# The kernels' transform of an S4D layer: last stage on sixteen 32x32 tiles, and its order on TensorE tied to the output projection's

## The chip, the cores and the metric

The kernel runs on one core of a Trainium2 chip. The metric is device time of one execution in microseconds, as the median of the runs shown. The profile's engine names are used: PE (TensorE's matmuls), PEld (its weight loads), DVE (VectorE), ACT (ScalarE), POOL (GpSimd), SP (SyncE, which here only starts transfers). All tensors in device memory are float32.

## The reference, cut to what matters

The input `x` is 2048 positions x 640 channels. Four layers run one after the other, attention and S4D in turn, with the same weights the second time:

```
x = x + MHA(LN(x))      # 32 heads of 20 channels, softmax, then @ wo (640 x 640)
x = x + S4D(LN(x))
x = x + MHA(LN(x))
x = x + S4D(LN(x))

S4D(u):  K[d, l] = 2 Re sum_n C[d,n] dt[d] exp(A[d,n] dt[d] l)   # 640 channels x 2048 positions, 128 states
         y = irfft(rfft(u, 4096) * rfft(K, 4096))[:2048] + u * D_skip
```

`K` hangs on the weights alone. It is computed once, its transform is computed once, and both S4D layers read that transform.

## The kernel before, in words

**Attention.** For each pair of heads, ScalarE's exponentials (`pt<-S`) stand between the score matmuls (`S`, line 858) and the value matmuls (`pa`, line 892). Results are copied to `oc`, normalised with `db` and stored to device memory in rows (`ot<-oc`, issued by POOL). In the first layer a generator, `kgen`, makes `K` (`kd` in device memory) piece by piece beside attention. The list `rest` holds the pieces of work that prepare the output projection; they run in attention's last stretch.

**Output projection** (`out_proj`). There are 16 rows `s` of 128 positions. A row is loaded as `otl`, split into a high and a low part (`oh`, `ol`), and multiplied with the split weights `woh`, `wol` in 30 matmuls of 128x320: ten of `ol` x `woh` (line 1307), then twenty of `oh` x `woh` and `wol` (line 1312), into two PSUM banks `po`. DVE adds a bank to `x`. Behind it comes the layer norm `ln_u` of a row or a group of rows, which makes `uh` and `ul`, the split input of the convolution.

**Kernels' transform** (`ktransform`, first layer only). This is the Fourier transform of `K`, in five blocks of 128 channels. It is a generator too. `filler` holds it, and `weave(n)` runs `n` of its pieces, up to its next `yield`. In a block:
1. `kl`, 128 channels x 2048 positions, is loaded from `kd`, `D_skip` is added to its first element, and 16 transposes (`pkt<-kl`, line 1244) turn it, split into halves `ktrh` (ACT) and `ktrl` (DVE).
2. First stage: eight groups of twelve f16 matmuls (`pkx`, line 1256), copied to `kx1`.
3. 32 transposes (`pkt<-kx`, line 1264), four at a time, copied with a scale to `kxt`.
4. Last stage: for every four transposes one f32 matmul of 128x512 (`pkf`, line 1272) with the matrix `f`. Two shuffles on DVE spread its 16-row halves over the partitions of `kn[0]` and `kn[1]`, ACT multiplies `kn[1]` by a sign (`sgn`), and for every second one two stores of 512 KB go to `kha` and `khb`.

Its constants `f`, `sgn` and `skip` and the tiles `ktr`, `kx1` lie in the pool `f1`, opened when the generator first runs; `kl`, `kxt` and `kn` have two buffers each in `f2`. A pool that takes memory which another pool has left waits for the last use of that pool.

**Order.** In row 2 of the output projection `weave(1000)` emits the whole transform at once. The scheduler of the framework then places each instruction on its engine by dependency and priority, so that on PE the transform and the projection's rows mix freely. `chain` (with `tie`) is how the program fixes an order by hand: an instruction that is tied stands behind the one tied before it on its engine. In before only `kgen` uses it. An engine runs its instructions strictly in the order in which they were placed.

**Convolution** (`ssm`). It transforms `uh`, `ul` (`psx`, line 1384, copied by ACT to `x1`), multiplies by `ka` and `kb`, which 160 transfers of 256 KB read from `kha` and `khb` in the two layers, and transforms back.

Of the kernel before, what the change touches and what calls it, by code (L numbers as in the profile page):

```python
# [21 lines left out]
P = 128  # L22
# [65 lines left out]
def mha_s4d_kernel(ctx, tc, x_in, wqkv, wo, lar, aim, cr, ci, ldt, dsk,  # L88
                   c_e1, c_eb, c_f2, c_fa, c_sel, c_lv, c_id, c_sg, c_e16, c_f16, c_id16, c_dn, out, parts="asas", general=None):
    nc = tc.nc  # L90
# [26 lines left out]
    wd = dram.tile([P, 3, len(LV), D], F32, name="wd")  # L117
    kha = dram.tile([P, D // 4, P], F32, name="kha")
    khb = dram.tile([P, D // 4, P], F32, name="khb")
    qs = dram.tile([2, D, L], F16, name="qs")  # L120
# [68 lines left out]
    def chain(ins):  # L189
        last[0] = tie(ins, last[0])  # L190

    def kgen():
# [954 lines left out]
    def prefetch(x, rest):  # L1147
# [42 lines left out]
        return x, c, woh, wol, w2  # L1190
    ups = []

# [15 lines left out]
    SWAP = list(range(16, 32)) + list(range(16))  # L1208
    DUP0 = list(range(16)) * 2
    DUP1 = list(range(16, 32)) * 2  # L1210

    def by_channel(x1, i2):
        return x1[:, :, i2].rearrange("p g (s c) -> p s g c", c=4)

    def ktransform(e1):

        c = ExitStack()
        c1 = c.enter_context(tc.tile_pool(name="f1", bufs=1))
        c2 = c.enter_context(tc.tile_pool(name="f2", bufs=2))
        f2 = c1.tile([P, P], F32, name="f2")  # L1220
        sy.dma_start(f2, c_f2)
        sgn = c1.tile([P, 1], F32, name="sgn")
        sy.dma_start(sgn, c_sg)

        skip = c1.tile([P, NCT], F32, name="skip")
        sy.dma_start(skip, dsk)

        def load(b):
            kl = c2.tile([P, L], F32, name="kl")
            sy.dma_start(kl, kd[b * P:b * P + P, :])  # L1230
            return kl
        kls = [load(0)]

        def unit_load(b):
            kl = kls.pop()
            if b + 1 < NCT:
                kls.append(load(b + 1))
            ve.tensor_add(kl[:, 0:1], kl[:, 0:1], skip[:, b:b + 1])
            hi, lo = (c1.tile([P, NI, P], F16, name=f"ktr{n}") for n in "hl")
            klv = kl.rearrange("d (p i) -> d i p", i=NI)  # L1240
            for i4 in range(4):
                pt = pst("T", [P, 4, P], F32, tag="T", name="pkt")
                for i in range(4):
                    te.transpose(pt[:, i, :], klv[:, 4 * i4 + i, :], ident)
# [3 lines left out]
                yield  # L1248
            x1 = c1.tile([P, 32, NI // 2, 16], F32, name="kx1")
            for i2 in range(NI // 2):  # L1250
                ps = pst("X", [P, 2, 2, P], F32, tag="X", name="pkx")
                for i in range(2):
                    s = 2 * i2 + i
                    for r in range(2):
                        for n, (e, m) in enumerate(((0, hi), (0, lo), (1, hi))):
                            te.matmul(ps[:, r, i, :], e1[:, e, s, r, :], m[:, s, :], start=(n == 0), stop=(n == 2))
                (ve.tensor_copy if i2 % 4 == 1 else se.copy)(by_channel(x1, i2), ps.rearrange("p r i (g c) -> p (r i) g c", c=4))
                yield
            prev = None
            for q in range(9):  # L1260
                if q < 8:
                    pt = pst("T", [P, 4, P], F32, tag="T", name="pkt")
                    for g in range(4):
                        te.transpose(pt[:, g, :], x1[:, 4 * q + g].rearrange("p i s -> p (i s)"), ident)
                    xt = c2.tile([P, 512], F32, name="kxt")
                    se.activation(xt, pt.rearrange("p g k -> p (g k)"), AF.Copy, scale=ksc[:, 1:2])
                if prev is not None:
                    g0 = b * 32 + 4 * (q - 1)
                    if q % 2:
                        kn = [c2.tile([P, 2, 512], F32, name=f"kn{s}") for s in range(2)]  # L1270
                    px = pst("F", [P, 512], F32, tag="F", name="pkf")
                    te.matmul(px, f2, prev, start=True, stop=True)  # L1272
# [3 lines left out]
                    if q % 2 == 0:  # L1276
                        for s, dst in enumerate((kha, khb)):
                            sy.dma_start(dst[:, g0 - 4:g0 + 4, :].rearrange("p g k -> p (g k)"),
                                         kn[s].rearrange("p q k -> p (q k)"))
                prev = xt  # L1280
                yield
        for b in range(NCT):
            yield from unit_load(b)
        c.close()

    def out_proj(x, woh, wol, rows, first, ln, load):
# [10 lines left out]
        feed()  # L1297
        due = []
        to_come = {s: 0 for s in range(NI)}
        for s, c0, c1 in rows.left + [e[0] for e in rows.loaded + first]:  # L1300
            to_come[s] += 1
        while first:
            (s, c0, c1), oh, ol = first.pop(0)
            pos = [pst("M", [P, 512], F32, tag="mm", name="po")[:, :320] for _ in range(2)]
            for hf in range(2):
                for ct in range(c0, c1):
                    te.matmul(pos[hf], ol[:, ct, :], woh[:, ct, 320 * hf:320 * hf + 320], start=(ct == c0), stop=False)  # L1307
            feed()
            for hf in range(2):
                for ct in range(c0, c1):  # L1310
                    for m in (woh, wol):
                        te.matmul(pos[hf], oh[:, ct, :], m[:, ct, 320 * hf:320 * hf + 320],  # L1312
                                  start=False, stop=(ct == c1 - 1 and m is wol))
# [17 lines left out]
        while due:  # L1331
            ln(*due.pop(0))


# [14 lines left out]
    def ssm(x, uh, ul, consts, last):  # L1349
# [19 lines left out]
        with ExitStack() as c:  # L1369
# [198 lines left out]
    def seq(x, general):  # L1568

        stats = None  # L1570
        for n in range(0, len(parts), 2):
            with ExitStack() as c:
# [9 lines left out]
                if n == 0 and not general:  # L1582
                    psum(c3, M=2, T=2, F=2)
                else:
# [47 lines left out]
def _constants():  # L1632
# [13 lines left out]
    for s, o, m in ((0, 0, C), (1, 0, S), (0, 1, -S), (1, 1, C)):  # L1646
        fa[:, s, :, :, o] = np.einsum("hli,cd->hlcid", m.reshape(4, 4, 16), e4)
    f2 = f2.reshape(2, NI // 2, 2, 4, P).transpose(1, 0, 2, 3, 4)
    sg = np.zeros((4, 2, 16, 1))
    sg[:, 0], sg[:, 1] = -1.0, 1.0  # L1650
# [5 lines left out]
    cs = dict(c_e1=e1.reshape(P, -1), c_eb=eb.reshape(P, -1), c_f2=f2.reshape(P, P), c_sg=sg.reshape(P, 1),  # L1656
              c_fa=fa.reshape(P, -1), c_sel=sel.reshape(P, -1), c_lv=lv, c_id=np.eye(P))
    cs = {n: np.ascontiguousarray(a.astype(np.float32)) for n, a in cs.items()}
    for n, a in (("c_e16", e1), ("c_f16", f2)):
# [10 lines left out]
_ORDER = ["x_in", "wqkv", "wo", "lar", "aim", "cr", "ci", "ldt", "dsk",  # L1670
          "c_e1", "c_eb", "c_f2", "c_fa", "c_sel", "c_lv", "c_id", "c_sg",
          "c_e16", "c_f16", "c_id16", "c_dn"]
# [30 lines left out]
```

## Time and profile before

| | |
|---|---|
| Median of 3 runs | 2675.46 us (2673.86 to 2678.34) |
| The profiled execution | 2680.85 us |
| Its span, and its mean granted clock | 2679.1 us, 0.996 |
| PE busy | 2530.0 us, 94% of the span |
| ACT busy | 2368.7 us, 88% |
| DVE busy | 1516.0 us, 57% |
| POOL busy | 827.7 us, 31% |
| Stage of the change: first `po` to first `psx` | 1102.90 to 1273.59 us |

How to read it: a busy share is a mean over stages with different limits, and matmuls overlap, so that a busy PE need not be at its peak. The 40 slices of the page are 67 us each; the stage of the change is in slices 17 to 20, counted from 1. In a row of instructions stand start and duration in us, engine, line, operation, output and inputs, and how many follow one another (x8); in brackets the idle time before it and what ended it. In a group stand busy time and mean ns, then idle time before and its releasers.

### The profile page before, as it was taken

Reading aid. Unit: us, or ns where it says so; the run is one execution under the profiler, and the core shown is the slowest. Engines: PE = TensorE matmul, PEld = TensorE weight load, DVE = VectorE, ACT = ScalarE, POOL = GpSimd, SP = SyncE. Lnnn points to the kernel's source line nnn. Section 1 sums busy time; section 2 is a strip of 40 time slices with the busy share of each in tenths; the row PEclk is TensorE's granted clock in tenths of the full one; section 3 lists DMA queues with packets and bytes.
Section 4 is the critical chain, followed back from the end, with each engine's and each line's share of the span. In section 5 each row is a group of like instructions: output and inputs, shape, how many; then the busy total and the mean of one; then the engine's idle time right before and its main releaser. Section 6 shows DMA issues by size and latency. Waiting matters only on the chain.

```text
span 2679.1 us, 116332 instructions
## 1 busy us (share of the span) xinstructions
PE 2530.0 (94%) x51106; PEld 1425.0 (53%) x51106; DVE 1516.0 (57%) x3451; ACT 2368.7 (88%) x2793; POOL 827.7 (31%) x1256
## 2 busy tenths in 40 slices
PE   7899999999999998899998999999999998999898
PEld 3445444444444443678896444454444443444788
DVE  8687777886855994477776333232233221154865
ACT  7889999999999999676655799999999999999564
POOL 1123323333323334301672122222222222222376
PEclk9999999999999999999999999999999999999999
DMA  6513222322221224364542121121121113222465
GB/s 210 181 49 86 67 76 55 87 55 76 52 61 49 54 68 155 110 233 162 189 151 69 40 59 50 50 58 47 45 65 38 54 30 93 69 67 60 145 190 162
DMA packets 186580, 242.18 MB, mean 90 GB/s; under 512 B 43376, under 2 KB 128976, under 8 KB 184400
## 3 DMA queue, kind: packets, MB, share of 16 engines
q1 hardware_dynamic: 150048, 188.35, 21.8%
q0 software_dynamic: 36016, 46.30, 7.0%
q8 instruction: 403, 6.60, 1.0%
q14 instruction: 113, 0.93, 0.1%
HBM read 158.50 MB, written 76.01 MB: 88 GB/s over the span
## 4 chain that ended last, share of the span: by engine, by line
ACT 52%; PE 25%; issue 10%; DVE 6%; DMA 3%; POOL 1%; SPq 0%; ACTq 0%; DVEq 0%; POOLq 0%
ACT pt L78 50%; PE pa L892 4%; PE psv L1419 3%; PE psy L1429 3%; PE S L858 3%; PE psx L1407 2%; PE m L611 1%; PE psx L1384 1%; PE po L1312 1%; DMA kop<-ks 1%; PE pst L1394 1%; PE pkf L1272 1%; DVE ktab L78 1%; PE po L1307 1%; PE pq L764 1%
## 5 line engine op out<-in xcount | busy, mean ns | idle before, releaser
L78 ACT ACTIVATE pt<-S 128x1024 f32<-128x1024 f32 x2048 | 1928.6, 1032 | 41.4 <-PE S L858 29.2
L892 PE MATMUL pa<-pt,V 64*32 64x512 f32 x16384 | 1100.9, 590 | 1.4 <-DVE oc L78 1.2
L858 PE MATMUL S<-qop,kop 61*32 61x512 f16 x16384 | 882.9, 381 | 85.2 <-ACT pt L78 68.4
L858 PEld LDWEIGHTS <-kop 61*32 61x32 f16 x16384 | 366.7, 89 | 741.1 <-issue 622.4
L892 PEld LDWEIGHTS pa<-pt,V 64*32 64x32 f32 x16384 | 315.1, 106 | 74.6 <-issue 9.7
L78 POOL DMA_DIRECT2D dn<-oc x252 | 124.5, 501 | 670.6 <-DVE oc L78 643.8
L78 DVE TENSOR_SCALAR qc<-m 128x512 f32<-128x512 f32 (+1 forms) x68 | 46.8, 689 | 303.6 <-PE m L611 303.6
L78 POOL DMA_DIRECT2D db<-dn x252 | 128.0, 514 | 135.1 <-DMA dn<-dr 132.1
L78 DVE COPY oc<-pa 128x512 f32<-128x512 f32 x64 | 44.1, 690 | 199.6 <-PE pa L892 191.9
L611 PE MATMUL m<-xh,wh 64*32 64x512 f16 x2560 | 147.9, 379 | 5.5 <-DVE qc L78 5.5
L78 POOL DMA_DIRECT2D ot<-oc x256 | 130.4, 516 | 71.6 <-DVE oc L78 42.8
L611 PE MATMUL m<-xh,wl 64*32 64x512 f16 x2560 | 148.1, 377 | 0.0
L611 PE MATMUL m<-xl,wh 64*32 64x512 f16 x2560 | 146.7, 376 | 0.0
L611 PEld LDWEIGHTS <-wh 64*32 64x32 f16 x5120 | 92.9, 93 | 78.4 <-issue 36.4
L78 ACT COPY xt<-pst 128x1024 f16<-128x1024 f16 x80 | 81.6, 1022 | 47.2 <-PE pst L1394 47.0
L1412 POOL TENSOR_TENSOR t<-t,kb 128x512 f32<-128x512 f32 x80 | 102.0, 1276 | 67.6 <-DVE t L78 66.7
L78 POOL DMA_DIRECT2D dn<-dr x63 | 35.3, 560 | 248.8 <-DVE dr L78 236.4
L78 DVE TENSOR_SCALAR V<-m 128x160 f32<-128x160 f32 x64 | 20.7, 324 | 158.5 <-PE m L577 158.5
L78 DVE TENSOR_TENSOR kb<-ktab 128x512 f32<-128x512 f32 x160 | 107.7, 692 | 0.0
L577 PEld LDWEIGHTS <-xh 128*128 128x128 f16 x960 | 79.7, 98 | 47.0 <-issue 31.6
L1413 POOL TENSOR_TENSOR t<-t,t 128x512 f32<-128x512 f32 x78 | 99.3, 1273 | 8.5 <-DVE t L78 2.6
L329 PEld LDWEIGHTS m<-kb,ka 128*32 128x32 f32 x3840 | 61.0, 109 | 72.1 <-issue 55.3
(305 smaller groups left out, 4020.7 us busy)
## 6 DMA issues: line engine op xcount, KB each, us to landing
ka<-kha SPq DMA_DIRECT2D x80, 256.0 KB
kb<-khb SPq DMA_DIRECT2D x80, 256.0 KB
db<-dn POOLq DMA_DIRECT2D x252, 64.0 KB, 2.6
kop<-ks SPq DMA_DIRECT2D x176, 80.0 KB
kpw<-wd POOLq DMA_DIRECT2D x60, 192.0 KB, 4.7
qop<-qs SPq DMA_DIRECT2D x256, 40.0 KB
ot<-oc POOLq DMA_DIRECT2D x256, 40.0 KB, 3.0
kha<-kn SPq DMA_DIRECT2D x20, 512.0 KB
```

What stands on the lines that cost most here:

```text
L78: made = f(out, *a, **k)
L329: chain(te.matmul(ps[32 * j:32 * j + 32, c8, :], a[n][:, ch, :], b[n][:, dd, :], start=(n == 0), stop=(n == 2), tile_position=(0, 32 * j)))
L577: chain(te.matmul(ps[:, :n], a_[:, ct, sl], m[:, ct, :], start=(k == 0), stop=(k == 14)))
L611: chain(te.matmul(ps[r][32 * t:32 * t + 32, :], a_[rows, ct, 32 * u:32 * u + 32], m[rows, ct, 512 * v:512 * v + 512], start=(k == 0), stop ...
L764: te.matmul(pq, a_[:, ct, :], m[:, ct, sl], start=(n == 0), stop=(n == 14))
L858: chain(te.matmul(S[32 * t:32 * t + 32, 512 * r:512 * r + 512], kt_[rows, kc + 32 * t:kc + 32 * t + 32], qt[rows, :], start=True, stop=Tru ...
L892: chain(te.matmul(pa[r][32 * j:32 * j + 32, :], V[rows, kt, VP * h:VP * h + 32], pts[j // 2][rows, 512 * (j % 2):512 * (j % 2) + 512], sta ...
L1407: te.matmul(px, f2[:, f, :], xt[:, k, :], start=(n == 0), stop=(n == 2))
L1412: ge.tensor_mul(t2, t2, kb)
L1413: (ge if g0 else ve).tensor_add(t1, t1, t2)
L1419: te.matmul(pv[:, g].rearrange("p r i c -> p (r i c)"), t1[:, g * P:g * P + P], fa, start=True, stop=True)
L1429: te.matmul(py[:, i, :], eb[:, 4 * i4 + i, r, :], v[:, r, 4 * i4 + i].rearrange("p g c -> p (g c)"), start=(r == 0), stop=(r == 1))
```

## The change

- **Last stage.** The matrix `f` becomes two matrices of 32x32, one for `kha` and one for `khb`, which already hold the doubling and the sign. For each block, each half `t` and each of the two, `ends` runs 16 matmuls of 32x32 tiles (`tile_position`) with 512 columns each into four PSUM banks (tags F0 to F3, one buffer each). DVE copies two banks and ACT two, into two `kn` tiles of 512 KB, each stored by one transfer. The shuffles, the sign multiplication and the load of `sgn` go. There are 20 `ends` in all.
- **Layouts.** `kx1` is laid out so that the transposes read every 32nd element. Channels are taken in the order (c g) instead of (g c): `kl` is loaded in four transfers of 32 partitions. `kha` and `khb` have a new shape, and the convolution's loads `ka`, `kb` read pieces of 512 B where they read pieces of 2 KB.
- **`kl`** has one buffer, `kl0`, in the pool `wo1`. Block 0 is loaded in attention's last stretch (from `rest`), each next one after the second half of the by-time transposes of the block before (`by_time(b, 1)`).
- **Copies.** Half of the `kx` copies go to DVE (a quarter before), and every fourth `kxt` copy too (none before).
- **Order on PE.** All the transform's matmuls and transposes are tied, and so are the projection's while the transform lives. After every seventh `po` matmul one piece of the transform is woven in (`mm`). `weave(1000)` moves from row 2 to behind the last layer norm. There are 480 `po` matmuls, so 68 pieces are woven, and the transform has 70.
- **PSUM.** In this stage 2 + 4 banks (M, F0 to F3) in place of 2 + 2 + 2 (M, T, F), beside the two of X, which the transposes now share with `pkx`.
- **Kernel generator.** One `yield` more for each `reduce_max`, and `bound` is queued behind `load_powers(2)`, with key 3 instead of 1.

```diff
     def kgen():
...
         for n, t in enumerate((ld["cr"], ld["ci"], skip)):
+            yield
             ve.reduce_max(big[:, n:n + 1], t, axis=AX.X, apply_absolute_value=True)
...
-        slow.append((1, bound))
         load_powers(2)
+        slow.append((3, bound))
...
         if rest:
+            kl0[:] = [w1.tile([P, L], F32, name="kl")]
+            rest.append(lambda: load_kl(0))
...
+    def load_kl(b):
+        for ch in range(4):
+            sy.dma_start(kl0[0][32 * ch:32 * ch + 32, :],
+                         kd[b * P:b * P + P, :].rearrange("(g c) l -> c g l", c=4)[ch])
...
-        f2 = c1.tile([P, P], F32, name="f2")
-        sy.dma_start(f2, c_f2)
-        sgn = c1.tile([P, 1], F32, name="sgn")
-        sy.dma_start(sgn, c_sg)
+        f2 = c1.tile([P, 2, 32], F32, name="f2")
+        sy.dma_start(f2, c_f2.rearrange("p (s m) -> p s m", s=2))
         skip = c1.tile([P, NCT], F32, name="skip")
-        sy.dma_start(skip, dsk)
+        sy.dma_start(skip, dsk.rearrange("(g c) n -> c g n", c=4))
...
+        def by_time(b, h):
+            kl = kls[0]
+            if h == 0:
+                ve.tensor_add(kl[:, 0:1], kl[:, 0:1], skip[:, b:b + 1])
+                hl[:] = [c1.tile([P, NI, P], F16, name=f"ktr{n}") for n in "hl"]
...
+            for i4 in (2 * h, 2 * h + 1):
...
+                    transpose(pt[:, i, :], klv[:, 4 * i4 + i, :], ident)
...
+            if h and b + 1 < NCT:
+                load_kl(b + 1)
...
-                (ve.tensor_copy if i2 % 4 == 1 else se.copy)(by_channel(x1, i2), ps.rearrange("p r i (g c) -> p (r i) g c", c=4))
+                (ve.tensor_copy if i2 % 2 else se.copy)(x1[:, :, i2].rearrange("p c s g -> p s c g"),
+                                                        ps.rearrange("p r i (c g) -> p (r i) c g", c=4))
+                if i2 % 2:
+                    yield
...
+            def ends(t, xt, s, dst):
+                px = [pst("F", [P, 512], F32, tag=f"F{ch}", name=f"pkf{ch}") for ch in range(4)]
+                for ch in range(4):
+                    rows = slice(32 * ch, 32 * ch + 32)
+                    for g in range(4):
+                        matmul(px[ch][32 * g:32 * g + 32, :].rearrange("p (q k) -> p q k", k=P), f2[rows, s, :],
+                               xt[rows, :, g, :], start=True, stop=True, tile_position=(32 * ch, 32 * g))
+                for h in range(2):
+                    kn = c2.tile([P, 2, 4, P], F32, name=f"kn{s}")
+                    for ch in range(2):
+                        (se.copy if ch else ve.tensor_copy)(kn[:, ch], px[2 * h + ch].rearrange("p (q k) -> p q k", k=P))
+                    sy.dma_start(dst[2 * b + t][:, 2 * h:2 * h + 2], kn)
+            xts = [c2.tile([P, 4, 4, P], F32, name="kxt") for t in range(2)]
+            steps = [(turned, 0, xts[0], 0), (turned, 0, xts[0], 1), (ends, 0, xts[0], 0, kha),
+                     (turned, 1, xts[1], 0), (ends, 0, xts[0], 1, khb), (turned, 1, xts[1], 1),
+                     (ends, 1, xts[1], 0, kha), (ends, 1, xts[1], 1, khb)]
+            if b + 1 < NCT:
+                steps.insert(7, (by_time, b + 1, 0))
+                steps.append((by_time, b + 1, 1))
...
-                    te.matmul(px, f2, prev, start=True, stop=True)
-                    for s in range(2):
-                        ve.stream_shuffle(kn[s][:, (q - 1) % 2, :], px, [DUP0, DUP1][s])
-                    se.activation(kn[1][:, (q - 1) % 2, :], kn[1][:, (q - 1) % 2, :], AF.Copy, scale=sgn)
...
     def out_proj(x, woh, wol, rows, first, ln, load):
...
+        def mm(*a, **k):
+            if filler[0] is None:
+                te.matmul(*a, **k)
+                return
+            matmul(*a, **k)
+            many[0] += 1
+            if many[0] % 7 == 0:
+                weave(1)
...
-                if s == 2:
-                    weave(1000)
...
         while due:
             ln(*due.pop(0))
-
+        weave(1000)
...
-                sy.dma_start(ka, kha[:, g0:g0 + 4, :].rearrange("p g k -> p (g k)"))
-                sy.dma_start(kb, khb[:, g0:g0 + 4, :].rearrange("p g k -> p (g k)"))
+                for t, src in ((ka, kha), (kb, khb)):
+                    sy.dma_start(t.rearrange("p (g k) -> p g k", k=P),
+                                 src[g0 // 16].rearrange("(g a) c q k -> (a c) g q k", g=4)[:, :, q % 4])
...
-                    psum(c3, M=2, T=2, F=2)
+                    psum(c3, M=2, F=1)
```

More of the change, by code (lines that the diff above doesn't have):

```diff
@@ L190, in chain, with matmul, transpose @@
         last[0] = tie(ins, last[0])
+    def matmul(*a, **k):
+        chain(te.matmul(*a, **k))
+    def transpose(*a, **k):
+        chain(te.transpose(*a, **k))
     def kgen():
@@ new lines, in block, with turned @@
+                            matmul(ps[:, r, i, :], e1[:, e, s, r, :], m[:, s, :], start=(n == 0), stop=(n == 2))
+                (ve.tensor_copy if i2 % 2 else se.copy)(x1[:, :, i2].rearrange("p c s g -> p s c g"),
+                                                        ps.rearrange("p r i (c g) -> p (r i) c g", c=4))
+                if i2 % 2:
+                    yield
+            def turned(t, xt, h):
+                for q in (2 * h, 2 * h + 1):
+                    pt = pst("X", [P, 4, P], F32, tag="X", name="pkt")
+                    for g in range(4):
+                        transpose(pt[:, g, :], x1[:, :, :, :, 16 * t + 4 * q + g].rearrange("p c i s -> p (c i s)"), ident)
+                    if q == 3:
+                        ve.tensor_scalar_mul(xt[:, q], pt, ksc[:, 1:2])
+                    else:
+                        se.activation(xt[:, q], pt, AF.Copy, scale=ksc[:, 1:2])
@@ L1282, in ktransform @@
+        for h in range(2):
+            by_time(0, h)
+            yield
         for b in range(NCT):
-            yield from unit_load(b)
+            yield from block(b)
         c.close()
@@ L1306, in out_proj @@
                 for ct in range(c0, c1):
-                    te.matmul(pos[hf], ol[:, ct, :], woh[:, ct, 320 * hf:320 * hf + 320], start=(ct == c0), stop=False)
+                    mm(pos[hf], ol[:, ct, :], woh[:, ct, 320 * hf:320 * hf + 320], start=(ct == c0), stop=False)
             feed()
@@ L1311, in out_proj @@
                     for m in (woh, wol):
-                        te.matmul(pos[hf], oh[:, ct, :], m[:, ct, 320 * hf:320 * hf + 320],
-                                  start=False, stop=(ct == c1 - 1 and m is wol))
+                        mm(pos[hf], oh[:, ct, :], m[:, ct, 320 * hf:320 * hf + 320],
+                           start=False, stop=(ct == c1 - 1 and m is wol))
                 xs = x[:, s, 320 * hf:320 * hf + 320]
                 ve.tensor_add(xs, xs, pos[hf])
-                if s == 2:
-                    weave(1000)
             to_come[s] -= 1
```

69 lines of the change are left out of this document (22 added, 47 removed).

## The prediction

> **What bounds the kernel now.** I read the page's 40 slices first, then busy time by stage, then the groups of instructions of the stage, then the chain and single instructions at its ends.
>
> ```profile
> ACT  7889999999999999676655799999999999999564
> 1102.90 1.73 PE L1307 MATMUL po<-woh,ol 128*128 128x320 f32 x10
> 1273.44 0.31 PE L1312 MATMUL po<-wol,oh 128*128 128x320 f32 x1
> 1273.59 0.23 PE L1384 MATMUL psx<-uh,e1s 128*128 128x128 f16 x1
> 1103.00:1133.00 30.00, 28.30 (x184) 26.92 (x184) 21.44 (x54) 11.78 (x17) 15.34 (x22) 1.00 0.49 154
> 1133.00:1253.00 120.00, 118.34 (x960) 91.71 (x961) 91.95 (x250) 92.85 (x150) 8.81 (x7) 1.00 0.57 216
> 1253.00:1274.00 21.00, 21.00 (x146) 20.39 (x146) 15.16 (x44) 8.56 (x14) 5.83 (x4) 1.00 0.15 50
> ```
>
> ScalarE sets the pace while it stands at 9 (attention's exponentials); it falls to 5–7 in slices 17 to 22. Into that gap falls the stage of the change: the first output projection with the kernels' transform, from the first `po` at 1102.90 to the first `psx` at 1273.59, 170.7 us. The three window rows (columns: length, then PE, weight loads, DVE, ACT, POOL with counts, granted clock, DMA share, GB/s) show PE full in it: 167.6 of 171 us, clock 1.00. The stage ends when PE has done its work; DVE has 128.6 us, ACT 113.2.
>
> PE's time per instruction comes from starts, since the ends of overlapping ones are modelled:
>
> ```profile
> 1190.37 1.09 PE L1264 MATMUL pkt<-ident,kx 128*128 128x128 f32 x8
> 1191.22 0.39 PE L1312 MATMUL po<-woh,oh 128*128 128x320 f32 x1
> 1148.37 0.86 PE pkf L1272 x2
> 1230.91 1.35 PE pkx L1256 x24
> 1248.20 2.92 PE po L1312 x20
> L1272 PE MATMUL pkf<-kxt,f 128*128 128x512 f32 x80 | 41.3, 608 | 0.0
> ```
>
> Eight transposes take 0.85 us to the next start (0.109 each over the stage), 24 `pkx` 1.35 (0.056), 20 `po` 2.92 (0.147), one last-stage matmul (two records: 80 records are 40 instructions) 0.86. Work: 480 x 0.147 = 70.6, 480 x 0.056 = 26.8, 240 x 0.109 = 26.2, 40 x 0.865 = 34.6, together 158.2. So 12.5 us of the 170.7 are waits.
>
> **The change part by part.**
>
> *Last stage.* 40 matmuls become 20 groups (`ends`) of 16 tiles, which fill four banks each. The nearest rows are attention's, where tiles of 64x32 run together:
>
> ```profile
> 2384.10 0.41 PE L858 MATMUL S<-qop,kop 61*32 61x512 f16 x8
> 2384.31 1.06 PE L892 MATMUL pa<-pt,V 64*32 64x512 f32 x16
> 2385.17 0.41 PE L858 MATMUL S<-qop,kop 61*32 61x512 f16 x8
> 2385.51 0.41 PE L1067 MATMUL m<-wol,oh 128*128 128x320 f32 x1
> 2386.30 0.41 PE L858 MATMUL S<-qop,kop 61*32 61x512 f16 x8
> ```
>
> Eight f32 tiles (16 records) take 0.86, as long as one full matmul. Sixteen take 0.865 if all run together, 1.72 in two lots; I take 0.865, since eight cost no more than one. Going from small tiles to full ones and back costs: from 2385.17 to 2386.30 are 1.13 us for an `S` group (0.21, from 2384.10 to 2384.31) and four projections (4 x 0.147 = 0.59), so 0.33 for the two switches. The Trainium skill, "TensorEngine Tiling (Array Packing)", Key Properties, says that a change of tiling mode drains TensorE; the 0.33 us agree, and it speaks against the change. An `ends` thus costs 1.20, twenty 23.9 against 34.6.
>
> *DVE and ACT.*
>
> ```profile
> L78 DVE STREAM_SHUFFLE kn<-pkf 128x512 f32<-128x512 f32 x80 | 54.2, 737 | 0.0
> L78 ACT ACTIVATE kn<-kn,sgn 128x512 f32<-128x512 f32 x40 | 28.3, 721 | 1.5 <-DVE kn L78 0.9 <-DVE va L78 0.2
> L78 ACT ACTIVATE kxt<-pkt,ksc 128x512 f32<-128x512 f32 x40 | 26.6, 677 | 8.8 <-PE pkt L1264 8.8
> L78 ACT COPY kx<-pkx 128x512 f32<-128x512 f32 x30 | 17.4, 584 | 6.4 <-PE pkx L1256 6.3
> L78 DVE COPY kx<-pkx 128x512 f32<-128x512 f32 x10 | 6.9, 686 | 3.2 <-PE pkx L1256 3.2
> ```
>
> DVE loses 80 shuffles x 0.737 = 59.0 and gains 60 copies (40 of `pkf`, 10 of `kx`, 10 of `kxt`) x 0.686 = 41.2. ACT loses 40 x 0.721 + 10 x 0.584 + 10 x 0.677 = 41.4 and gains 40 x 0.584 = 23.4. Both get 18 us lighter. Neither bound the stage, so this is worth nothing by itself. Stride-32 reads by the transposes: 0, since the by-time ones already read at a stride of 16 elements at about the same price (eight in 1.14 at 1133.46 below, 1.09 at 1190.37 above). The stores of `kn` keep their number and size: 0. The next block's `kl` now has one buffer: its four loads go out when the block's second by-time piece is done, and it is needed some ten pieces, over 15 us, later; 1 MB at the stage's 216 GB/s takes 5 us, so it is hidden, and without that cover four blocks would cost 5 each.
>
> *The tied order.* This decides. Now the transform is emitted at row 2, and PE takes whichever of both is ready. Afterwards every PE instruction of the stage has its place, and the first piece of the transform stands behind the seventh `po`. When could it start?
>
> ```profile
> 1122.14 1.28 DVE L78 TENSOR_TENSOR oc<-oc,db 128x512 f32<-128x512 f32 x1 [0.28 <-DMA db<-dn]
> 1121.47 3.22 POOL L1206 TENSOR_TENSOR ul<-u,uh 128x640 f16<-128x640 f32 x2 [1.39 <-ACT uh L78]
> 1124.64 2.04 POOL L78 DMA_DIRECT2D ot<-oc  x4
> SPq L78 <- DMA ot<-oc: 3.2, 1, 3.2
> 1129.63 0.35 SPq L78 DMA_DIRECT2D f<-in_c_f  x1
> 1130.03 0.61 SPq L78 DMA_DIRECT2D sgn<-in_c_sg  x1
> 1130.69 0.43 SPq L78 DMA_DIRECT2D skip<-in_dsk  x1
> 1132.57 0.86 DVE L78 TENSOR_TENSOR kl<-kl,skip 128x1 f32<-128x1 f32 x2
> 1133.46 1.14 PE L1244 MATMUL pkt<-ident,kl 128*128 128x128 f32 x8 [0.47 <-issue]
> ```
>
> The transform's constants wait on SP (3.2 us) for attention's last `ot<-oc` stores, whose memory their pool `f1` reuses; `skip` goes out at 1130.69, it is added to `kl`, and the first transposes run at 1133.46. Before that PE did 184 `po`. The change moves `kl` out of this pool, but not `f` and `skip`, and the first piece needs `skip`. So PE stops after seven `po` (1102.90 + 7 x 0.147 = 1103.9) and resumes about when the transform starts now. Two things make that earlier: POOL's `ul` before the stores is not there (no row is finished), so they can go at 1123.4, not 1124.64; and the `sgn` load between `f` and `skip` (0.66) is gone. 1133.46 less 1.2, 0.66 and about 0.4 of `kl` adds shared with a second block: 1131.2. The hold is 27.3 us.
>
> From there all 473 other `po` and the transform remain: 473 x 0.147 = 69.5, 26.2, 26.8, and 18 `ends` x 1.20 = 21.5 (two come behind the last row): 144.0. After a hold the clock is lower for a while:
>
> ```profile
> 1430.00:1433.00 3.00, 0.00 (x0) 0.00 (x0) 3.00 (x8) 2.65 (x7) 0.00 (x0) 1.00 0.03 4
> 1433.00:1436.00 3.00, 2.46 (x9) 1.20 (x10) 3.00 (x6) 2.90 (x5) 0.00 (x0) 0.70 0.49 137
> 1436.00:1440.00 4.00, 4.00 (x16) 1.66 (x15) 2.45 (x6) 2.63 (x7) 0.00 (x0) 0.80 0.00 0
> ```
>
> Behind an idle stretch the granted clock was 0.70, then 0.80: 0.3 x 3 + 0.2 x 4 = 1.7 us. The Trainium skill, "TensorE: Matmul & The Clock Gate", Part 1, states half rate for about 3.4 us; by it an estimated 1.7, the same. A fixed order also waits where a copy is late: 68 pieces each follow one whose copies take 0.58 to 0.74, with seven `po` (1.03) between. I put 6 us on this, between 0 and the 12.5 us of waits that the free order leaves now. The last `po` ends at 1131.2 + 144.0 + 1.7 + 6 = 1282.9, against 1273.6: +9.3.
>
> *Behind the last row.* Two `ends`, their copies and stores come last, and the convolution's buffers reuse that memory:
>
> ```profile
> 1175.88 4.39 DMA khb<-kn
> 1275.84 0.56 ACT L78 CAST x<-psx 128x512 f16<-128x512 f32 x1
> ```
>
> Now `psx` is first copied 2.3 us behind the last `po`; then it must wait for two `ends` (2.4), a copy and a landing (4.4), some 8 us, after which bunched copies recover part. I take +2.5, between 0 (all recovered) and +6 (nothing).
>
> *The convolution's loads*, in rows of 512 B instead of 2 KB:
>
> ```profile
> q1 hardware_dynamic: 11789, 23.10, 49.5%
> q1 hardware_dynamic: 19010, 26.65, 59.9%
> SPq L78 <- POOL t L1412: 80.6, 36, 3.8
> ```
>
> In 1275 to 1420 a packet of 1959 B on average took 97 ns (0.495 x 145 us x 16 / 11789); in 2520 to 2660 one of 1402 B took 71. On a line through both 512 B take 28: four cost 111 for 97, and the share rises to about 56%. SP waits 80.6 us there for free buffers, which covers it: 0, at most 14% of 72 us of DMA time, 10 us, if nothing covers it.
>
> *Into attention's last stretch* go four loads of `kl` and some yields of the kernel generator. ACT at 9 hides them; without that cover four issues cost SP under 2 us.
>
> **Sum:** +9.3 + 2.5 = +11.8 on the profiled execution's 2680.85: 2692.6. Its runs' median is 2675.46, 5.4 less: 2687.
>
> **The rivals.**
>
> *No hold (faster).* If `f` and `skip` don't wait for attention's stores, PE goes through from 1102.90: 70.6 + 26.2 + 26.8 + 21.5 + 6 = 151.1, end at 1254.0, −19.6, with the tail −17: 2658. For it: the pool is laid out anew. Against: it shrinks by 0.7 KB only. Every us of hold costs one, so 17 us of hold, that is `skip` added before about 1121, is where it decides.
>
> *Held, but nothing else waits.* No handover waits, tail recovered: +3.3, 2679. For it: DVE and ACT have slack. Against: even the free order waits 12.5 us.
>
> *Tiles in two lots.* 18 x 0.865 = 15.6 more: 2703. Here the change's saving on PE turns into a loss. Against: eight tiles ran as one. The Trainium skill's clock-gate page, Part 3, has sixteen such tiles running as one; no row here shows sixteen.
>
> *Loads bound the convolution.* Up to 10 us in each of two layers: about 2697 to 2707.
>
> **How the numbers follow.** About 0.2% (5.4 us) is what a measurement of this kernel can tell from no change. Hold with waits: 0.50, own range 2681 to 2700. No hold: 0.20. Held only: 0.17. Two lots: 0.10. Loads: 0.03. Time 2687. The range 2656 to 2704 takes in the no-hold case, which alone holds 0.20, and the two lots. Faster: no hold, 0.20. Same: held only, 0.17. Slower: the rest, 0.63.
>
> **What would show it.** Hold: PE idle from about 1104 to 1131 behind seven `po`, released by DVE's `kl`, while SP's load of `f` waits for `ot<-oc`. Tiles: a `pkf` group of 32 records in 0.87 plus 0.33, or in 1.72. Waits: PE's idle time by releaser from there to the last `po`, 6 us; last `po` near 1283. Tail: first `x<-psx` 8 us behind it. Loads: `ka` and `kb` in the chain, or SP still waiting on POOL. The forecast is wrong if PE isn't held for more than 17 us, whatever the rest does.

## The result, and the profile after

The changed kernel took 2712.09 us (median of 4, 2711.27 to 2713.23) against 2675.53 for the kernel before: ratio 1.0133, interval 1.0118 to 1.0147, slower by 36.6 us where 11.5 were forecast and 2704 was the upper end. In the two profiled executions (2711.27 and 2680.85) the difference is 30.4 us, since the one of before lies 5.3 us above its median. Where they part is read from three tiles, before first, after second (first and last start of the group):

```profile
L1307 PE MATMUL po<-woh,ol x160: 302/309/418, 1102.9 to 1270.5; 128*128 128x320 f32 x160
L1312 PE MATMUL po<-wol,oh x160: 302/309/393, 1104.6 to 1273.4; 128*128 128x320 f32 x160
L1429 PE MATMUL psy<-v,eb x320: 275/275/377, 1314.4 to 1424.8; 128*128 128x128 f32 x160
```

```profile
L193 PE MATMUL po<-woh,ol x160: 302/309/616, 1099.4 to 1286.5; 128*128 128x320 f32 x160
L193 PE MATMUL po<-wol,oh x160: 302/309/615, 1128.4 to 1293.0; 128*128 128x320 f32 x160
L1466 PE MATMUL psy<-v,eb x320: 275/275/377, 1344.5 to 1454.9; 128*128 128x128 f32 x160
```

From the first `po` to the last: 170.5 us before, 193.6 after (+23.1). From the last `po` to the first `psy`, the convolution's output: 41.0 and 51.5 (+10.5). From the first `psy` to the last: 110.4 both times. Attention ended 3.5 us earlier. Sum: +30.1, so nearly all of the 30.4 arises in the stage and just behind it.

The hold is there, as PE's timeline, SP's waits and the chain show:

```profile
1099.43 1.29 PE L193 MATMUL po<-woh,ol 128*128 128x320 f32 x7
1125.58 1.97 PE L196 MATMUL pkt<-ident,kl 128*128 128x128 f32 x8 [24.86 <-DVE kl L78]
SPq L78 <- DMA ot<-oc: 5.8, 1, 5.8
1120.40 1.79 DMA ot<-oc
1122.82 2.03 DMA skip<-in_dsk
```

Seven `po`, then 24.86 us of nothing until attention's last store has landed, `skip` is loaded and added to `kl`. Behind it PE's waits by releaser, and its clock in some stretches (columns as in the prediction):

```profile
PE pkx L193 <- DVE ktrl L78: 5.6, 2, 4.8
PE psx L1420 <- DVE x L78: 4.6, 1, 4.6
PE pkx L193 <- ACT kx L78: 2.4, 2, 1.2
PE pkf L193 <- ACT kxt L78: 2.0, 1, 2.0
PE po L193 <- DVE x L78: 1.0, 3, 0.5
PE pkf L193 <- DVE va L78: 0.8, 1, 0.8
PE pkt L196 <- ACT kxt L78: 0.6, 1, 0.6
PE pkf L193 <- DVE rs L78: 0.3, 1, 0.3
```

```profile
1120.00:1130.00 10.00, 4.42 (x20) 4.38 (x21) 2.39 (x4) 1.37 (x2) 0.90 (x2) 0.51 0.09 18
1230.00:1240.00 10.00, 5.93 (x52) 5.73 (x53) 3.41 (x6) 4.67 (x8) 2.75 (x2) 0.66 0.77 175
1300.00:1310.00 10.00, 5.42 (x55) 4.94 (x52) 2.12 (x4) 2.64 (x5) 0.00 (x0) 0.67 1.05 415
```

The longest of these waits, 4.78 us at 1234, is spelled out by ACT's timeline:

```profile
1229.67 1.73 ACT L78 ACTIVATE u<-x,nb,rs 128x640 f32<-128x640 f32 x2 [1.28 <-DVE nb L78]
1231.31 1.33 ACT L78 CAST uh<-u 128x640 f16<-128x640 f32 x2
1232.55 1.25 ACT L78 ACTIVATE ktrh<-pkt,ksc 128x512 f16<-128x512 f32 x2
1234.07 0.29 PE L193 MATMUL pkx<-ktrh,e1s 128*128 128x128 f16 x1 [4.78 <-DVE ktrl L78]
```

The layer norm of two rows (`u`, `uh`) stands ahead of the transform's copy on ACT. PE, whose next instruction is fixed, waits for that copy, though the `po` placed behind it don't need its result.

### The profile page after: what moved, and what is told of

Read it like the earlier page. It is cut to its first block, busy times and chain, and to the rows that moved or that the text cites. A ratio compares the mean times of both kernels' runs of the same rounds, so it can differ in the third digit from the quotient of the medians.

```text
span 2709.5 us, 117355 instructions
## 1 busy us (share of the span) xinstructions
PE 2527.4 (93%) x51666; PEld 1425.9 (53%) x51666; DVE 1497.3 (55%) x3351; ACT 2352.7 (87%) x2773; POOL 822.9 (30%) x1256
## 4 chain that ended last, share of the span: by engine, by line
ACT 49%; PE 26%; issue 10%; DVE 6%; DMA 4%; POOL 1%; SPq 0%; ACTq 0%; DVEq 0%; POOLq 0%
ACT pt L78 48%; PE pa L899 5%; PE S L865 3%; PE psv L1456 3%; PE psy L1466 2%; PE po L193 2%; PE psx L1444 2%; PE m L618 2%; PE psx L1420 2%; PE pst L1430 1%; DMA kop<-ks 1%; PE pkx L193 1%; PE m L335 1%; PE pkt L196 1%; DVE ktab L78 1%
## 5 line engine op out<-in xcount | busy, mean ns | idle before, releaser
L78 DVE COPY oc<-pa 128x512 f32<-128x512 f32 x64 | 44.1, 690 | 190.9 <-PE pa L899 183.3
```

What stands on the lines that cost most here:

```text
L78: made = f(out, *a, **k)
```

## The experiments

Theory T: the fixed order is the loss, in four parts: the hold, copies that come late (ACT's queue, the clock behind it), the switching between kinds of work, and the two groups left behind the last row. Rivals: the tiles with their single PSUM banks cost it; or a fixed order keeps its waits whatever is repaired. On the chips of these runs the kernel before took 2679 to 2681 us, so ratios are compared. The changed kernel itself ran on the first chip alone. Stage is from the first to the last `po`, tail from there to the first `psy`, both in us and from one profiled execution of each kernel (that of e13 lies 8.8 us above its median):

| run | ratio to before | interval | stage | tail |
|---|---|---|---|---|
| before | 1 | | 170.5 | 41.0 |
| changed kernel | 1.0133 | 1.0118–1.0147 | 193.6 | 51.5 |
| e1_pool_swapped | 1.0131 | 1.0114–1.0148 | 183.8 | 50.1 |
| e2_late_weave | 1.0070 | 1.0054–1.0087 | 188.3 | 41.0 |
| e3_untied | 1.0030 | 1.0018–1.0041 | 178.6 | 41.0 |
| e4_before_tied | 1.0171 | 1.0154–1.0188 | 214.4 | 42.9 |
| e6_norm_on_pool | 1.0094 | 1.0077–1.0111 | 182.7 | 51.4 |
| e7_late_norm_on_pool | 1.0048 | 1.0031–1.0064 | 180.7 | 41.2 |
| e8_before_norm_on_pool | 1.0055 | 1.0038–1.0071 | 183.3 | 41.8 |
| e9_untied_norm_on_pool | 1.0038 | 1.0025–1.0051 | 175.4 | 43.2 |
| e10_early_consts | 1.0011 | 1.0002–1.0020 | 172.2 | 39.1 |
| e11_untied_norm_dve | 1.0018 | 1.0009–1.0026 | 170.3 | 40.4 |
| e12_before_kgen | 1.0006 | 0.9997–1.0014 | 173.5 | 41.0 |
| e13_before_norm_dve | 0.9999 | 0.9991–1.0008 | 175.7 | 40.6 |
| e14_repaired_late | 1.0010 | 1.0001–1.0019 | 168.9 | 42.2 |
| e17_hold_only | 1.0092 | 1.0074–1.0111 | 184.1 | 48.7 |
| e18_repaired_late_norm_act | 1.0027 | 1.0017–1.0037 | 177.6 | 40.9 |

**The hold.**

```diff
-        c1 = c.enter_context(tc.tile_pool(name="f1", bufs=1))
         c2 = c.enter_context(tc.tile_pool(name="f2", bufs=2))
+        c1 = c.enter_context(tc.tile_pool(name="f1", bufs=1))
```

> The changed kernel with the pools f1 and f2 created in the other order, so that the constants f and skip (f1) lie on memory that attention's last stores don't read; f2 lies there instead. Theory (the hold is the price): the 24.9 us in which PE waits for kl+skip go, and a shorter one appears where the first kxt (f2) is written, about 7 pieces or 16 us after the first po, so 5 us of hold stay: 20 us less than the changed kernel, about 2692. Rival (the hold only moves on, since the woven order meets the same store one piece later): less than 8 us gained, 2704 or more.

Measured: 1.0131. The hold went (seven `po` at 1115.22, the first transposes at 1116.36), but attention lost more:

```profile
SPq L78 <- DMA kd<-ko: 22.0, 1, 22.0
1070.00:1080.00 10.00, 2.40 (x48) 0.90 (x47) 0.00 (x0) 4.66 (x6) 2.03 (x4) 0.77 1.03 269
1084.43 2.72 PE L899 MATMUL pa<-pt,V 64*32 64x512 f32 x16 [11.15 <-DVE oc L78]
```

The load of `f` now waited 22 us for the generator's last stores (`kd<-ko`), and behind it on SP stood attention's own loads (`qop`) and then `x` and `kl`. These two went out at 1062 to 1066 rather than 1043 to 1047, the DMA engines were full (share 1.03), and `oc` was 11 us late. By its number (less than 8 us gained) the rival holds, but not for its reason, so the run says nothing clean about the hold. The next edit moves no load of attention:

```diff
+            kl0[:] = [w1.tile([P, L], F32, name="kl"), w1.tile([P, 2, 32], F32, name="f2"),
+                      w1.tile([P, NCT], F32, name="skip")]
+            def consts_kl():
+                load_kl(0)
+                sy.dma_start(kl0[1], c_f2.rearrange("p (s m) -> p s m", s=2))
+                sy.dma_start(kl0[2], dsk.rearrange("(g c) n -> c g n", c=4))
+            rest.append(consts_kl)
```

(and the two pools swapped as above, with `f2, skip = kl0[1:]` in place of their loads).

> The changed kernel with the hold alone repaired: f and skip beside kl in wo1 and loaded behind it, f1 off attention's output buffers; a piece for every 7 po from the start, norm on ACT, two pieces left behind the last row. Theory (the hold of 24.9 us is a price, but the pieces that now run earlier meet attention's last output): no wait at kl, 8 to 12 us of new waits in the first 35 us, so 13 to 17 us less than the changed kernel: ratio 1.007 to 1.009. Rival A (the whole hold is gained): ratio 1.004. Rival B (what the hold cost comes back as other waits): ratio 1.011 or more.

Measured: 1.0092, 0.41% or 11 us less than the changed kernel. The theory's band ended at 1.009, rival B began at 1.011; both lie inside the interval. Of 24.9 us about 11 are gained; the rest comes back mostly as waits on attention's last output, and 2.6 us as a wait for the constant `e1s`, whose load goes out at 1100.38, when attention's last `pa` has ended:

```profile
PE pkx L193 <- DVE kx L78: 6.3, 1, 6.3
PE pkt L196 <- ACT kxt L78: 3.5, 2, 3.0
PE pkx L193 <- DMA e1s<-in_c_e: 2.6, 1, 2.6
```

**Starting late**, so that 184 `po` cover the hold:

```diff
-            if many[0] % 7 == 0:
+            if many[0] > 184 and many[0] % 4 == 0:
```

> The changed kernel, but weaving starts only after 184 po matmuls (27 us of po) and then takes one piece for every 4 po, so that all 70 pieces lie ahead of the last row. Theory (hold and tail are the price, the fixed order costs some waits): the hold is covered by po (25 us less), and the last stores of kn land earlier (about 8 us less behind the last po); 2679, and up to 10 us more for waits. Rival (the fixed order itself is the price: 0.59 us of po between two pieces don't cover a piece's copies of 0.6 to 1.4 us): the waits of 11.9 us grow by 20 or more, 2700 or above.

Measured: 1.0070, 17 us less than the changed kernel, 2694 on the first chip's scale: between the two. The tail came back whole (51.5 to 41.0). The stage gained only 5.3 us, since in place of the hold the waits grew from 11.9 to 25.7 us, and two more groups lie in it:

```profile
PE pkx L193 <- DVE ktrl L78: 9.0, 4, 4.9
PE pkx L193 <- ACT kx L78: 5.4, 4, 2.6
```

**The order alone.** e4 ties before's own transform:

```diff
-                if s == 2:
-                    weave(1000)
+            matmul(*a, **k)
+            many[0] += 1
+            if many[0] % 9 == 0:
+                weave(2)
```

(the last lines in the projection's `mm`, as in the change; the transform's matmuls and transposes are tied too).

> The kernel before (full matmuls, shuffles, kl in f2), with only the order tied: every po is tied, two pieces of the transform (105 in all) are woven after every ninth po, what is left behind the last norm. Theory (the order is the loss): a hold of 25 to 30 us from the first weave on, some 10 us of waits, and the tail: 2705 to 2720. Rival (the tiles are the loss): within 8 us of before, 2668 to 2684.

Measured: 1.0171, worse than expected and worse than the changed kernel. No tile is in it, and the hold is the same (the profile names no releaser of PE, but the transposes start behind the addition of `skip`, as in the changed kernel):

```profile
PE pkt L196 <- issue: 24.4, 1, 24.4
1130.26 0.23 DVE L78 TENSOR_TENSOR kl<-kl,skip 128x1 f32<-128x1 f32 x2 [6.57 <-DMA skip<-in_dsk]
PE pkf L193 <- ACT kxt L78: 11.5, 9, 3.2
```

So the order alone loses 46 us. The changed kernel loses 10 us less (1.0133): that is what the tiles gain inside a tied order together with its other parts, the copies, the place of `kl`, and one piece at a time instead of two, which no run separates.

**The tiles alone.** e3 takes the tie off the changed kernel:

```diff
     def matmul(*a, **k):
-        chain(te.matmul(*a, **k))
+        te.matmul(*a, **k)
...
-            if many[0] % 7 == 0:
-                weave(1)
...
+                if s == 2:
+                    weave(1000)
```

> The changed kernel with its tiles, layouts and transfers, but with the order of before: nothing of the transform or the projection is tied, and the transform is emitted at row 2. Theory (the order is the whole loss, the tiles a gain): PE has 20 x 1.26 = 25 us in place of 34.6 for the last stage, so 5 to 10 us less than before: 2665 to 2671. Rival (the tiles, four single PSUM banks and two shared ones cost it): no faster than before, 2680 to 2705.

Measured: 1.0030; most of the loss is gone, as the theory says, but the gain is not there, as the rival says. Untied, the scheduler puts groups of tiles close together, and each must wait until its four single banks are copied out. PE's clock and timeline, and ACT's:

```profile
1174.00:1176.00 2.00, 1.52 (x8) 0.20 (x8) 0.66 (x1) 2.00 (x4) 2.00 (x2) 0.50 0.78 317
1178.00:1180.00 2.00, 2.00 (x10) 1.84 (x8) 1.58 (x2) 0.18 (x1) 0.00 (x0) 0.50 0.74 297
1174.47 1.93 PE L193 MATMUL pkf<-kxt,f 32*32 32x512 f32 x8 [0.64 <-ACT kn L78]
1170.49 1.73 ACT L78 ACTIVATE u<-x,nb,rs 128x640 f32<-128x640 f32 x2 [1.42 <-DVE nb L78]
1172.59 1.35 ACT L78 CAST uh<-u 128x640 f16<-128x640 f32 x2
```

The same norm on ACT stands between the copies, PE runs eight records at a time, and the granted clock falls to 0.50. Counted from each group's first start to the next other instruction, the 20 groups took 34.7 us here, against 35.2 for before's 40 matmuls; in e2 and e14, where they stand apart, 22.1. Counted in the same way, 7.0 of the 8.1 us by which e3's stage is longer lie in the transposes (33.4 against 26.4).

**The norm off ACT.** `on_pool`, set for the first layer, puts `u` and `uh` on POOL for all rows but two:

```diff
+            if on_pool and s < NI - 2:
+                ge.tensor_scalar(u, x[:, s, :], mv[:, i, 0:1], rs[:, i:i + 1], ALU.subtract, ALU.mult)
...
+            (ge.tensor_copy if on_pool and s < NI - 2 else se.copy)(uh[:, s, :], u)
```

> The changed kernel with the layer norm's u and uh of the first layer (all rows but the last two) on POOL instead of ACT. Theory (behind the hold, PE's waits come from ACT's queue, where u and uh of two rows, 3.1 us, stand ahead of the transform's copies): the waits of 11.9 us behind the hold fall below 4, and of 4 us lost to the clock the second half goes: 8 to 11 us less than the changed kernel, ratio to before about 1.010. Rival (the waits come from the copies' own latency in a fixed order, whatever else is on ACT): less than 3 us, ratio 1.012 to 1.014.

Measured: 1.0094, 10 us less than the changed kernel. The other waits of the transform's and the projection's matmuls fell from 12.7 us (the rows above without `psx`) to 5.0, and the stage is 10.9 us shorter; the hold stayed:

```profile
PE pkt L196 <- DVE kl L78: 25.4, 1, 25.4
PE pkx L193 <- DVE ktrl L78: 2.6, 4, 1.0
```

The theory holds here. With late weaving, untied, and on the kernel before it did less:

> The changed kernel with late weaving (from 184 po on, a piece for every 4 po) and the norm's u and uh on POOL. Theory: of some 26 us of waits that late weaving alone left on PE, 15 or more go, so that it lands within 5 us of before: ratio 0.998 to 1.002 (late weaving alone 1.007). Rival (4 po don't cover a piece's copies): the waits stay above 18 us, ratio 1.005 or more.

Measured: 1.0048 against 1.0070; the rival is nearer (waits still about 21 us).

> The changed kernel untied, emitted at row 2, with the norm's u and uh on POOL. Theory (untied, an ends took about 1.75 us instead of 1.2 since its four single banks wait for copies that stand behind u and uh on ACT, and the clock fell to 0.5 behind it): an ends comes down to 1.2 to 1.3 and no clock is lost, 10 to 14 us less than untied alone, ratio 0.997 to 0.999 to before. Rival (the four single banks are short whatever ACT does): 1.5 us or more for an ends, ratio 1.001 to 1.003.

Measured: 1.0038. The 20 groups came down from 34.7 to 27.7 us, 1.39 each, and the clock stayed at 1.00 from 1160 to the end of the stage, but the time didn't fall: PE waited for the rows instead (3.9 us for `x`, 0.6 in e3). Neither side.

> The kernel before with the norm's u and uh on POOL. Theory (PE's free order already covers what ACT is late with): within 4 us of before, ratio 0.9985 to 1.0015. Rival (ACT's queue costs the free order as well): 6 us or more faster, ratio below 0.998.

Measured: 1.0055, slower, which neither expected. The groups of instructions of this run point at the reason:

```profile
L1202 POOL TENSOR_SCALAR u<-x,mv,rs 128x640 f32<-128x640 f32 x14 | 36.9, 2642 | 100.2 <-DVE rs L78 57.7 <-issue 41.7 <-POOL ul L1208 0.8
L78 DVE TENSOR_SCALAR va<-mv 128x2 f32<-128x2 f32 x7 | 5.3, 756 | 0.2
```

POOL needs 2.64 us for what ACT does in 0.92, and five of DVE's seven kinds of small operations on 128x2 took 226 to 756 ns where they take 150 to 166 in before (`va`: 158). So from here on `u` is on DVE (608 ns in e11) and only `uh` on POOL (`off` is set for the first layer):

```diff
-            if on_act:
+            if on_act and not off:
                 se.activation(u, x[:, s, :], AF.Identity, scale=rs[:, i:i + 1], bias=nb[:, i:i + 1])
             else:
                 ve.tensor_scalar(u, x[:, s, :], mv[:, i, 0:1], rs[:, i:i + 1], ALU.subtract, ALU.mult)
-            se.copy(uh[:, s, :], u)
+            (ge.tensor_copy if off and s < NI - 2 else se.copy)(uh[:, s, :], u)
```

> The kernel before with the norm's u of the first layer on DVE and its uh on POOL. Theory (with both on POOL it lost 0.55% because POOL's u takes 2.64 us and slows DVE; PE's free order else covers ACT's queue): within 4 us of before, ratio 0.9985 to 1.0015. Rival (any norm work off ACT delays the rows in this order): 8 us or more slower, ratio above 1.003.

Measured: 0.9999: before's order neither loses nor gains by the norm's place, and with `u` off POOL the loss of e8 is gone.

> The changed kernel untied, emitted at row 2, with the norm's u on DVE and its uh on POOL (in the run with both on POOL one u took 2.64 us there and DVE's small operations beside it 0.5 to 0.76 us in place of 0.16). Theory: with neither ACT nor POOL late, an ends comes to 1.3 us and the stage to 165 us (178.6 untied alone, 170.5 before): ratio 0.997 to 0.999. Rival (the four single banks are the limit): an ends of 1.4 or more, ratio 1.000 to 1.003.

Measured: 1.0018, the rival: 20 groups in 28.2 us, 1.41 each, with nothing late on ACT. The stage, 170.3, is as long as before's. Seven us were saved on these groups (35.2 in before). Counted from start to next start, 5.4 of them are lost again in the transposes (31.8 against 26.4) and 1.4 in `po`. The transposes now share two banks with `pkx` where before had four for both; that this is what makes them slower is not shown.

**All repaired.** e10 has e17's constants and pools, e13's norm and its own weaving; e14 differs from it by the second line; e18 is e14 with the norm on ACT (`off` never set).

```diff
-            if many[0] % 7 == 0:
+            if many[0] > 24 and many[0] % 6 == 0:
...
+            if many[0] > 120 and many[0] % 5 == 0:
```

> The changed kernel with all the suspected costs taken away: f and skip lie beside kl in the pool wo1 and are loaded right behind it, f1 (ktr, kx1) lies off attention's output buffers (f2 lies on them), the norm's u of the first layer is on DVE and its uh on POOL, and weaving takes a piece for every 6 po from the 25th on, so that it ends some 36 po ahead of the last. Theory (hold 24.9, late copies 11.9 and the clock behind them, tail 10.5 are what the order cost): no hold at kl, at most 5 us at the first kxt; about 153 us of PE work plus 8 of waits from the first po, and the distance from the last po to the first psy as in before (41 us): ratio to before 0.994 to 0.998. Rival (a fixed order has waits of 20 to 25 us whatever is repaired, as in the runs without the hold): ratio 1.001 to 1.006.

Measured: 1.0011, at the rival's lower end. The tail is whole, the hold gone. The waits that stay lie at the start; PE's and DVE's timelines:

```profile
1120.06 0.26 PE L193 MATMUL pkx<-ktrh,e1s 128*128 128x128 f16 x1 [5.93 <-DVE kx L78]
1119.00 0.17 DVE L78 TENSOR_SCALAR dr<-dr 128x16 f32<-128x16 f32 x1 [7.38 <-DMA dr<-dn]
1109.40 1.72 SPq L78 DMA_DIRECT2D kl<-kd  x4
```

DVE waits for attention's last `dr`, and the copy of `kx` stands behind it. `dr` comes 7.7 us after its load was issued, behind the 1 MB of the second `kl`; in e14, where that `kl` is loaded later, 2.3 us.

> The run with everything repaired, but weaving from the 121st po on, a piece for every 5 po, so that the first pieces don't meet attention's last output (its division and stores end 23 to 30 us behind the first po). Theory (a tied order costs little once each woven piece finds its data there; in the repaired run 14 of its 15 us of waits lay in the first 60 us, on attention's last output): at most 8 us of waits in the stage, last po 161 us behind the first, 41 us to the first psy: ratio to before 0.994 to 0.997. Rival (the fixed order itself keeps 15 us or more of waits, wherever it starts): ratio 1.000 to 1.004.

Measured: 1.0010: the rival's band, though the waits of the stage, 10.4 us, lie between the two. The stage fell to 168.9, shorter than before's; the tail is 1.2 us longer. Stage and tail together are thus 0.4 us shorter than in before, and yet this execution is 3.9 us longer. The time is lost far behind the change, in the second attention (before, then e14; first and last start of `S`):

```profile
L858 PE MATMUL S<-qop,kop x8192: 372/377/631, 1490.4 to 2469.9; 61*32 61x512 f16 x200
L865 PE MATMUL S<-qop,kop x8192: 372/377/631, 1489.7 to 2472.9; 61*32 61x512 f16 x200
```

It took 979.5 and 983.2 us, with the same code.

> As the run before in this list, but with the norm's u and uh on ACT as in the changed kernel. Theory (u and uh of two rows ahead of the copies cost PE some 10 us of waits and clock): 8 to 12 us more than with the norm off ACT, ratio 0.998 to 1.001. Rival (with the hold gone the norm on ACT costs nothing): within 3 us of it.

Measured: 1.0027, 0.17% or 4.5 us more than e14 (stage 8.7 us longer in the profiles, of which 4.3 lie in the groups of tiles): between the two. ACT's queue does cost something without the hold too.

**The kernel generator.**

```diff
-        slow.append((1, bound))
         load_powers(2)
+        slow.append((3, bound))
...
         for n, t in enumerate((ld["cr"], ld["ci"], skip)):
+            yield
```

> The kernel before with the kernel generator's part of the change alone (a yield more at each reduce_max, bound behind load_powers and with key 3). Theory (it is what brought the first po of the changed kernel forward from 1102.9 to 1099.4): 2 to 4 us faster, ratio 0.9985 to 0.9993. Rival (that shift is only how executions differ): within 1 us, ratio 0.9996 to 1.0004.

Measured: 1.0006, first `po` at 1103.1: no gain. In the runs above the first `po` lay between 1099.4 and 1105.3 whatever the edit (e1 apart), so the 3.5 us of the changed kernel's profile are not explained by this part.

## Why the prediction was wrong, point by point

The sign was right, and so was the mechanism of the hold: PE stood behind seven `po` until `skip` came, behind attention's last store. The rival without the hold did not occur. Two terms of the sum failed, the handover waits in the stage and the time behind the last row: the forecast had +9.3 and +2.5, the profile has +23.1 and +10.5.

- **The hold.** 27.3 forecast, 24.86 measured; PE resumed at 1125.6 rather than 1131.2, 3.5 us of which are the earlier start. This step held, and erred on the other side.
- **The tiles.** The group at 1145 and what follows:

```profile
1145.40 1.14 PE L193 MATMUL pkf<-kxt,f 32*32 32x512 f32 x32
1146.47 1.29 PE L193 MATMUL po<-woh,ol 128*128 128x320 f32 x7
1147.60 1.04 PE L196 MATMUL pkt<-ident,kx 128*128 128x128 f32 x8
1148.40 0.40 PE L193 MATMUL po<-woh,oh 128*128 128x320 f32 x1
1148.64 0.30 PE L193 MATMUL po<-wol,oh 128*128 128x320 f32 x1
```

  1.07 us to the next start, 0.09 ahead of it and 0.10 more on the first `po` behind: 1.26 for 1.20. The two lots did not occur; the Trainium skill's "TensorE: Matmul & The Clock Gate", Part 3, by which sixteen such tiles run as one, agrees: they took 1.07 us, not twice 0.86.
- **Handover waits, forecast 6 us: the term that was mis-sized.** From 1125.58 to the last `po` are 167.6 us, where 151.7 were forecast. The waits are 11.9. The clock took 4.1, not 1.7: 2.77 us of work took 4.76 from 1125.58 on, and 2.75 took 5.05 from 1234.07 on (0.2 of this is counted in the next item). And an item was missing: the first `po` behind another kind takes 0.24 (1148.40 to 1148.64), not 0.147. At 50 returns beside those of the tiles that is 4.5. With 1.1 for the tiles these make 5.9 + 2.4 + 4.5 + 1.1 = 13.9 of the 15.9. Two of the 18 groups took 1.76 and 1.61 us instead of 1.07 (from 1191.99 and 1288.96 on), 1.2 more; 0.8 us are not assigned. The bound of this term rested on a misreading: the 12.5 us of the kernel before are not waits. By the prediction's own window rows PE was idle there for 3.4 us, and its waits of 0.2 us or more add up to 2.7; most of the rest lies at such changes of kind, which the prices per instruction left out. The error was to call DVE and ACT unbinding by their sums. In a fixed order the place of a copy in ACT's queue counts: e6 took the norm out of it and gained 10 us.
- **Behind the last row, forecast 2.5 (bound 6), measured 10.5.** The copies of `psx` start 14.75 us behind the last `po` (2.4 in before), not 8:

```profile
1293.04 0.31 PE L193 MATMUL po<-wol,oh 128*128 128x320 f32 x1
1295.56 4.87 PE L193 MATMUL pkf<-kxt,f 32*32 32x512 f32 x32 [0.79 <-DVE va L78]
1301.11 6.43 DMA khb<-kn
1307.79 2.05 ACT L78 CAST x<-psx 128x512 f16<-128x512 f32 x4 [6.71 <-DMA khb<-kn]
```

  The second left-over group took 4.87 us instead of 1.2, since with nothing between them it waited bank by bank for copies (its four banks start at 1295.56, 1296.32, 1297.62 and 1298.50). The last store took 6.43 us at a DMA share of 1.05, not 4.39. And of the 12.4 us by which the copies are later, only 1.9 were recovered; PE then had a clock of 0.67 (1300 to 1310) and 0.79 (1310 to 1320). Every tied run that ended the transform ahead of the last row (e2, e7, e10, e14, e18) had a tail of 39 to 42, and those that left two groups behind it (e1, e6, e17) 49 to 51.
- **The break-even "every us of hold costs one"** failed too: in e17 24.9 us less hold gave 11. The hold also covered the wait for attention's last output, into which the transform runs when it starts earlier.
- **At nothing, and right:** the loads of 512 B (110.4 us of convolution before and after) and stride-32 transposes (eight take 0.80 us to the next start, from 1147.60 to 1148.40, and 0.85 in before).
- **Not asked by the prediction:** whether the new last stage gains at all without the tie. e3 and e11 say no: in e3 the groups take as long as before's matmuls, and in e11 what they save is lost in the transposes and `po`. Tied and apart (e14) they save 13 us (22.2 against 35.2); waits (10.4 us against 2.7) and more returns to `po` from other work (70 against 38) take most of it back.

Shown are the hold, ACT's part in the waits, the tail, and that the tied order is what loses most: 46 us on the kernel before (e4), 28 of the changed kernel's 36.6 (e3). Open is why no repaired version beats before. e14 has 10 us of waits left, which may be moved further, but this was not tried. And a loss outside the stage is neither shown nor ruled out: the second attention took 978.4 to 980.9 us in the five profiles of kernels with before's transform (mean 979.8) and 979.7 to 986.2 in the twelve with the tiles (mean 982.1).

## What to carry to other kernels

Tying the order of a full engine gives up what hides every late input: before tying, list for each piece what its first instruction waits for and when that arrives, down to a small constant in a pool that reuses memory, and which other work stands ahead of its copies on their engine. Slack as a sum over the stage doesn't answer that. A gain on the bounding engine that costs PSUM buffers is to be tried untied and tied before both are changed at once.

## What the runs showed of the hardware that was not expected

- The granted clock fell to 0.50 (e3, 1174 to 1180) although PE's longest wait there was 0.64 us. Just before, a group ran in lots of 8, 16 and 8 records, started at 1171.44, 1172.74 and 1174.47; that these short stops in a row did it is inferred. The Trainium skill's "TensorE: Matmul & The Clock Gate", Part 1, on short idle stretches between groups that wait for PSUM, agrees.
- A `tensor_scalar` of 128x640 took POOL 2.64 us, ACT's form 0.92 and DVE's 0.61, and in the run with this work on POOL (e8) DVE's `va` on 128x2 took 756 ns where it takes 158 in before.
- The first f32 matmul of 320 columns behind another kind of work took 0.24 us to the next start, 0.09 more than in a row of its own kind.
